# Forming the complex product with the filters outside TensorE, so that the way back takes one TensorE product per slot

## The chip, the cores and the metric

One core of a Trainium2 chip runs the kernel. The metric is the device time of one execution in microseconds, lower is better; a run's time is the median of its executions. A profile shows one execution, and its span is about 1.8 us shorter than the time of that execution, since it counts from the first to the last instruction. Times by stage below come from the profiles, totals from the timed runs. The profiled execution of the kernel before was some 3 us slower than its median, so differences of spans and of times are not quite the same.

## The reference

```python
# x (8, 3008, 256); filt_r, filt_i (1505, 256); w_in (256, 2048), w_out (2048, 256), both float64 in DRAM
X = np.fft.rfft(x, axis=1)
Y = X * (filt_r + 1j * filt_i)[None]
y = np.fft.irfft(Y, n=3008, axis=1).astype(np.float32).reshape(24064, 256)
h = y @ w_in
return ((h - np.tanh(h)) @ w_out).astype(np.float32)
```

It is a filter in the frequency domain along the sequence, then a dense layer with the function h - tanh(h) between its two matrices. All TensorE work is in float32.

## The kernel before

The sequence index is n = 47 q + r. The transform is one of length 64 over q ("first", product pf), a transposition through DRAM, then for each of 32 frequency slots a product over r (pz), the multiplication with the filters (uv), and a product back over b (pe), another transposition through DRAM, and the way back over a (pu). Real and imaginary parts lie side by side in the partitions: 47 + 47 = 94 rows. Four pairs of batches go through this; while the dense layers of one pair run (ph, po), the next pair's transforms stand between them. Only the first pair's have nothing to hide behind.

```python
    def load_a2(p, k):                                   # 94 rows from DRAM
        t = sb.tile([R2, BD], F32, tag="a2", bufs=2, name="a2")
        nc.sync.dma_start(t, dram(ct1[p], k * BD, [[NK * BD, R2], [1, BD]]))
        return t

    def middle(p):
        a2 = {0: load_a2(p, 0)}
        waiting = []

        def back():
            k, uv = waiting.pop(0)
            pe = ps.tile([128, 2, DM], F32, tag="z", bufs=2, name="pe")
            for f in range(2):                           # two products of the way back
                nc.tensor.matmul(pe[0:R2], g3[:, (2 * k + f) * R2:(2 * k + f + 1) * R2],
                                 uv[:, f], start=(f == 0), stop=(f == 1))
            e1 = sb.tile([R2, 2, DM], F32, tag="e1", bufs=2, name="e1")
            nc.scalar.copy(e1, pe[0:R2])
            nc.scalar.dma_start(
                dram(ct2[p], k * R2 * DM, [[DM, R2], [NQ * NR * DM, 2], [1, DM]]), e1)

        for k in range(NK):
            # ... next a2 is loaded ...
            pz = ps.tile([128, 2, DM], F32, tag="z", bufs=2, name="pz")
            nc.tensor.matmul(pz[0:R2], f2[:, k * R2:(k + 1) * R2], a2.pop(k),
                             start=True, stop=True)
            uv = sb.tile([R2, 2, 2, DM], F32, tag="uv", bufs=2, name="uv")
            for f in range(2):
                nc.vector.tensor_mul(
                    uv[:, f], pz[0:R2],
                    filt[:, f, k, :].unsqueeze(1).to_broadcast([R2, 2, DM]))
            waiting.append((k, uv))
            if len(waiting) > 1:
                back()
            yield

    # the start: the first pair's transforms, and the loads of what stays
    parts = [0, 4, 16, NK]
    for a, z in zip(parts, parts[1:]):
        nc.scalar.dma_start(f2[:, a * R2:z * R2], f2_d[:, a * R2:z * R2])
        nc.scalar.dma_start(g3[:, 2 * a * R2:2 * z * R2], g_d[:, 2 * a * R2:2 * z * R2])
        load_filters(a, z)                               # on GpSimd's queue
    for _ in fs[0]:
        pass
    # ...
    ws = weights()            # 32 jobs: load 128x256 float64 weights, convert them on VectorE
    for _ in ms[0]:
        next(ws, None)        # one conversion per slot, in the order of the text
```

## Time and profile before

| | before |
|---|---|
| time | 3473.27 us (3472.45 to 3473.28, 3 runs) |
| first stage, to the first product pz | 204.8 us |
| first pair's middle, from there to the first dense product ph | 265.1 us |
| from the first dense product to the end ("streaming stage") | 3004.6 us |

The last three rows are the stages. Their limits are read from the timeline of TensorE: the start of the first record of pz and of ph.

```profile
204.78 1.99 PE L269 MATMUL pz<-a,f_sb 94*94 94x512 f32 x2 [14.34 <-DMA a<-ct]
469.85 7.22 PE L311 MATMUL ph<-ut,w_in_sb 128*128 128x512 f32 x16
```

Columns are the start, the length, the engine and line, what it makes from what, the forms, the count of records, and in brackets how long the engine had been idle and what ended that. So at 204.78 TensorE had waited 14.34 us for the first load of a. The span of 3474.5 less 469.85 is the streaming stage. How the page of this kernel is read for its bounds is in the prediction.

### The profile page before, as it was taken

Reading aid. Unit: us, or ns where it says so; the run is one execution under the profiler, and the core shown is the slowest. Engines: PE = TensorE matmul, PEld = TensorE weight load, DVE = VectorE, ACT = ScalarE, POOL = GpSimd, SP = SyncE. Lnnn points to the kernel's source line nnn. Section 1 sums busy time; section 2 is a strip of 40 time slices with the busy share of each in tenths; the row PEclk is TensorE's granted clock in tenths of the full one; section 3 lists DMA queues with packets and bytes.
Section 4 is the critical chain, followed back from the end, with each engine's and each line's share of the span. In section 5 each row is a group of like instructions: output and inputs, shape, how many; then the busy total and the mean of one; then the engine's idle time right before and its main releaser. Section 6 shows DMA issues by size and latency. Waiting matters only on the chain. (4 is left out here: it accounts for less than half of the span.)

```text
span 3474.5 us, 36231 instructions
## 1 busy us (share of the span) xinstructions
PE 3219.2 (93%) x10800; PEld 1985.4 (57%) x10800; DVE 2744.9 (79%) x4466; ACT 1946.3 (56%) x3441; POOL 1333.2 (38%) x855
## 2 busy tenths in 40 slices
PE   1256689999999999999999999999999999999998
PEld 0011146666666666666666666666666666666665
DVE  2243158888888888888888888888888999999998
ACT  0000046665555666665555666665555666666665
POOL 2100024443333444443333444444333444445453
PEclk9955589999999999999999999999999999999999
DMA  5631122201111012201111112111111100000000
GB/s 116 143 119 63 50 80 73 69 26 47 43 45 37 32 54 85 63 29 48 47 41 34 32 59 86 47 37 41 48 40 36 35 17 19 19 19 19 17 13 11
DMA packets 107702, 168.44 MB, mean 48 GB/s; under 512 B 17120, under 2 KB 65992, under 8 KB 107124
## 3 DMA queue, kind: packets, MB, share of 16 engines
q1 hardware_dynamic: 37776, 82.39, 7.9%
q10 hardware_dynamic: 50496, 52.68, 4.5%
q0 software_dynamic: 19232, 31.04, 2.9%
q8 instruction: 85, 1.39, 0.2%
q14 instruction: 113, 0.93, 0.1%
HBM read 92.00 MB, written 73.92 MB: 48 GB/s over the span
## 5 line engine op out<-in xcount | busy, mean ns | idle before, releaser
L322 POOL TENSOR_SCALAR large<-u 128x512 uint8<-128x512 f32 (+1 forms) x768 | 1271.5, 1656 | 1973.3 <-ACT u L320 1933.1
L343 PE MATMUL po<-w_out_sb,gt 128*128 128x256 f32 x6016 | 1423.8, 380 | 11.3 <-ACT ot L350 7.4
L311 PE MATMUL ph<-ut,w_in_sb 128*128 128x512 f32 (+1 forms) x3072 | 1418.5, 583 | 0.0
L343 PEld LDWEIGHTS po<-w_out_sb,gt 128*128 128x128 f32 x6016 | 1138.2, 190 | 483.1 <-issue 283.9
L320 ACT ACTIVATE u<-ph 128x512 f32<-128x512 f32 (+1 forms) x768 | 451.6, 588 | 825.3 <-issue 301.0
L311 PEld LDWEIGHTS ph<-ut,w_in_sb 128*128 128x128 f32 x3072 | 578.0, 190 | 453.3 <-issue 399.7
L323 DVE TENSOR_TENSOR gt<-ph,u 128x512 f32<-128x512 f32 (+1 forms) x768 | 518.3, 675 | 272.3 <-ACT th L321 271.4
L330 DVE COPY_PREDICATED gt<-large,th 128x512 f32<-128x512 uint8 (+1 forms) x768 | 586.2, 763 | 68.2 <-DVE gt L327 2.7
L327 DVE SCALAR_TENSOR_TENSOR gt<-sb,gt 128x512 f32<-128x512 f32 (+1 forms) x768 | 539.6, 703 | 65.5 <-DVE gt L327 1.8
L326 ACT ACTIVATE sa<-u,bias 128x512 f32<-128x512 f32 (+1 forms) x768 | 548.8, 715 | 0.0
L326 ACT ACTIVATE sb<-u,bias 128x512 f32<-128x512 f32 (+1 forms) x768 | 546.4, 711 | 0.0
L327 DVE SCALAR_TENSOR_TENSOR gt<-sa,gt 128x512 f32<-128x512 f32 (+1 forms) x768 | 518.9, 676 | 0.0
L329 DVE TENSOR_TENSOR th<-ph,th 128x512 f32<-128x512 f32 (+1 forms) x768 | 513.4, 668 | 0.0
L321 ACT ACTIVATE th<-ph 128x512 f32<-128x512 f32 (+1 forms) x768 | 449.5, 585 | 0.0
L258 PE MATMUL pe<-uv,g_sb 94*94 94x512 f32 x512 | 299.5, 714 | 61.7 <-ACT e L261 60.8
L261 ACT COPY e<-pe 94x512 f32<-94x512 f32 x128 | 74.4, 581 | 406.8 <-PE pe L258 215.7
L273 DVE TENSOR_TENSOR uv<-pz,filt_sb 94x512 f32<-94x512 f32 x256 | 171.5, 680 | 164.1 <-PE pz L269 164.1
L237 PE MATMUL pf<-x_sb,wf_sb 128*128 128x512 f32 x192 | 121.4, 725 | 151.8 <-ACT a L239 134.4
L258 PEld LDWEIGHTS pe<-uv,g_sb 94*94 94x94 f32 x512 | 93.3, 188 | 242.4 <-issue 135.3
L269 PE MATMUL pz<-a,f_sb 94*94 94x512 f32 x256 | 160.1, 711 | 24.7 <-DMA a<-ct 19.8
L239 ACT COPY a<-pf 128x512 f32<-128x512 f32 x96 | 55.4, 577 | 200.8 <-DMA ct<-a 134.2
L237 PEld LDWEIGHTS pf<-x_sb,wf_sb 128*128 128x128 f32 x192 | 39.5, 224 | 198.0 <-ACT a L239 166.4
(34 smaller groups left out, 536.2 us busy)
## 6 DMA issues: line engine op xcount, KB each, us to landing
a<-ct SPq DMA_DIRECT2D x128, 188.0 KB
ct<-e ACTq DMA_DIRECT2D x128, 188.0 KB
x_sb<-in_x_dram SPq DMA_DIRECT2D x92, 256.0 KB
ct<-a ACTq DMA_DIRECT2D x92, 256.0 KB
e<-ct SPq DMA_DIRECT2D x44, 512.0 KB
out_dram<-ot POOLq DMA_DIRECT2D x44, 512.0 KB, 3.0
w<-in_moe_w_in_dram SPq DMA_DIRECT2D x16, 256.0 KB
w<-in_moe_w_out_dram SPq DMA_DIRECT2D x16, 256.0 KB
```

Source lines behind the costliest of these rows:

```text
L258: nc.tensor.matmul(pe[0:R2], g3[:, (2 * k + f) * R2:(2 * k + f + 1) * R2], uv[:, f], start=(f == 0), stop=(f == 1))
L273: nc.vector.tensor_mul(uv[:, f], pz[0:R2], filt[:, f, k, :].unsqueeze(1).to_broadcast([R2, 2, DM]))
L311: nc.tensor.matmul(ph[:, 0:n], w_in[:, h, t * 128:(t + 1) * 128], uts[i][:, h, 0:n], start=(h == 0), stop=(h == 1))
L320: nc.scalar.activation(u, ph, AF.Square)
L321: nc.scalar.activation(th, ph, AF.Tanh)
L322: nc.gpsimd.tensor_single_scalar(out=large, in_=u, scalar=SMALL, op=ALU.is_ge)
L323: nc.vector.tensor_mul(gt, ph, u)
L326: nc.scalar.activation(sq, u, AF.Square, bias=bias, scale=s)
L327: nc.vector.scalar_tensor_tensor(out=gt, in0=sq, scalar=v, in1=gt, op0=ALU.add, op1=ALU.mult)
L329: nc.vector.tensor_sub(th, ph, th)
L330: nc.vector.copy_predicated(gt, large, th)
L343: nc.tensor.matmul(po[i][:, j, :], gt[:, j * 128:(j + 1) * 128], w_out[:, t, :], start=(t == 0 and j % 2 == 0), stop=(t == NT - 1), skip_g ...
```

## The change

With Z = zr + i zi and F = fr + i fi, the kernel before let VectorE make all four real products (zr fr, zi fi, zr fi, zi fr) and TensorE add them up, with two matrices g for two operands. The change forms (zr fr - zi fi, zr fi + zi fr) first and lets TensorE multiply once. For this the parts move to partitions 0 and 64: ScalarE copies pz to zs, swapped and half negated, VectorE multiplies pz with fr, GpSimd multiplies zs with fi and adds the two. Padding partitions must not hold garbage, so the filters' padding is set to zero by VectorE ahead of the filter loads.

```diff
-    f2 = cst.tile([R2, NK * R2], F32, name="f2_sb")
-    g3 = cst.tile([R2, NK * 2 * R2], F32, name="g_sb")
+    f2 = cst.tile([R2, NK * 128], F32, name="f2_sb")
+    g3 = cst.tile([IM + NR, NK * R2], F32, name="g_sb")        # 111 rows, half the columns
-    filt = cst.tile([R2, 2, NK, DM], F32, name="filt_sb")
+    filt = cst.tile([128, 2, NK, DM], F32, name="filt_sb")
 ...
     def load_filters(a, z):
+        for p0 in (32, 96):
+            nc.vector.memset(filt[p0:p0 + 32, :, a:z, :], 0.0)
 ... (the filters' rows at partitions 0 and 64 in place of 0 and 47; the same bytes)
     def back():
-            for f in range(2):
-                nc.tensor.matmul(pe[0:R2], g3[:, (2 * k + f) * R2:(2 * k + f + 1) * R2],
-                                 uv[:, f], start=(f == 0), stop=(f == 1))
+            nc.tensor.matmul(pe[0:R2], g3[:, k * R2:(k + 1) * R2], uv[0:IM + NR],
+                             start=True, stop=True)
 ...
-            nc.tensor.matmul(pz[0:R2], f2[:, k * R2:(k + 1) * R2], a2.pop(k),
+            nc.tensor.matmul(pz, f2[:, k * 128:(k + 1) * 128], a2.pop(k),
                              start=True, stop=True)
-            uv = sb.tile([R2, 2, 2, DM], F32, tag="uv", bufs=2, name="uv")
-            for f in range(2):
-                nc.vector.tensor_mul(
-                    uv[:, f], pz[0:R2],
-                    filt[:, f, k, :].unsqueeze(1).to_broadcast([R2, 2, DM]))
+            uv = sb.tile([128, 2, DM], F32, tag="uv", bufs=2, name="uv")
+            zs = sb.tile([128, 2, DM], F32, tag="zs", bufs=2, name="zs")
+            both = [128, 2, DM]
+            nc.scalar.mul(zs[0:IM], pz[IM:128], -1.0)
+            nc.scalar.copy(zs[IM:128], pz[0:IM])
+            nc.vector.tensor_mul(uv, pz, filt[:, 0, k, :].unsqueeze(1).to_broadcast(both))
+            nc.gpsimd.tensor_mul(zs, zs, filt[:, 1, k, :].unsqueeze(1).to_broadcast(both))
+            nc.gpsimd.tensor_add(uv, uv, zs)
 ... (the constant matrices change to match; comments fall away)
```

More of the change, by code (lines that the diff above doesn't have):

```diff
@@ L26 @@
 HI = NR - LO
+IM = 64
 DFF = 2048
@@ L75, in _consts @@
     f2[31, 1::2, NR] = w32.real.T[:, HI]
+    f2w = np.zeros((NK, R2, 128))
+    f2w[:, :, 0:NR], f2w[:, :, IM:IM + NR] = f2[:, :, :NR], f2[:, :, NR:]
     ctw = np.exp(2j * np.pi * np.outer(np.arange(33), np.arange(NR)) / SEQ)
-    g = np.zeros((NK, 2, R2, R2))
+    g = np.zeros((NK, IM + NR, R2))
     for a in range(31):
@@ L82, in _consts @@
         tr, ti = t1.real.T[perm, :], t1.imag.T[perm, :]
-        g1, g2 = g[a, 0], g[a, 1]
-        g1[:NR, :NR], g1[:NR, NR:] = tr, ti
-        g1[NR:, :NR], g1[NR:, NR:] = -tr, -ti
-        g2[:NR, :NR], g2[:NR, NR:] = -ti, tr
-        g2[NR:, :NR], g2[NR:, NR:] = -ti, tr
-        g2[LO:NR, :] *= -1.0
-        g2[NR + LO:R2, :] *= -1.0
+        g[a, :NR, :NR], g[a, :NR, NR:] = tr, ti
+        g[a, IM:, :NR], g[a, IM:, NR:] = -ti, tr
+    g[:, IM + LO:] *= -1.0
     t0 = (wr.conj() * ctw[0][:, None] / SEQ).T
     t32 = (wr.conj() * ctw[32][:, None] / SEQ).T
-    g1, g2 = g[31, 0], g[31, 1]
-    g1[0, :NR] = t0.real[0]
-    g1[NR, NR:] = t32.real[HI]
-    g1[1:LO, :NR], g1[NR + 1:NR + LO, :NR] = 2 * t0.real[1:LO], -2 * t0.real[1:LO]
-    g2[1:LO, :NR], g2[NR + 1:NR + LO, :NR] = -2 * t0.imag[1:LO], -2 * t0.imag[1:LO]
-    g1[LO:NR, NR:], g1[NR + LO:R2, NR:] = 2 * t32.real[0:HI], -2 * t32.real[0:HI]
-    g2[LO:NR, NR:], g2[NR + LO:R2, NR:] = -2 * t32.imag[0:HI], -2 * t32.imag[0:HI]
+    g[31, 0, :NR] = t0.real[0]
+    g[31, IM, NR:] = t32.real[HI]
+    g[31, 1:LO, :NR], g[31, IM + 1:IM + LO, :NR] = 2 * t0.real[1:LO], -2 * t0.imag[1:LO]
+    g[31, LO:NR, NR:], g[31, IM + LO:, NR:] = 2 * t32.real[0:HI], -2 * t32.imag[0:HI]
     w = np.exp(2j * np.pi * np.outer(np.arange(NQ), np.arange(33)) / NQ)
@@ L112, in _consts @@
         wf1,
-        f2.transpose(1, 0, 2).reshape(R2, NK * R2),
-        g.transpose(2, 0, 1, 3).reshape(R2, NK * 2 * R2),
+        f2w.transpose(1, 0, 2).reshape(R2, NK * 128),
+        g.transpose(1, 0, 2).reshape(IM + NR, NK * R2),
         s2)]
@@ L154, in load_filters @@
         n = min(z, NK - 1) - a
-        for v, srcs in enumerate(((filt_r, filt_i), (filt_i, filt_r))):
-            for p0, src in zip((0, NR), srcs):
+        for p0 in (32, 96):
+            nc.vector.memset(filt[p0:p0 + 32, :, a:z, :], 0.0)
+        if z == NK:
+            for p0 in (0, IM):
+                nc.vector.memset(filt[p0:p0 + 1, 1, NK - 1], 0.0)
+        for v, src in enumerate((filt_r, filt_i)):
+            for p0 in (0, IM):
                 nc.gpsimd.dma_start(
@@ L162, in load_filters @@
                     dram(src.tensor, (NQ - 1 - a) * DM, [[NQ * DM, HI], [-DM, n], [1, DM]]))
-            if z < NK:
-                continue
-            k = NK - 1
-            p_re, p_im = (0, NR) if v == 0 else (NR, 0)
-            nc.gpsimd.dma_start(filt[p_re:p_re + LO, v, k, :],
-                                dram(filt_r.tensor, 0, [[NQ * DM, LO], [1, DM]]))
-            nc.gpsimd.dma_start(filt[p_im:p_im + 1, v, k, :],
-                                dram(filt_r.tensor, SEQ // 2 * DM, [[DM, 1], [1, DM]]))
-            nc.gpsimd.dma_start(filt[p_im + 1:p_im + LO, v, k, :],
-                                dram(filt_i.tensor, NQ * DM, [[NQ * DM, LO - 1], [1, DM]]))
-            for p0, src in ((p_re, filt_r), (p_im, filt_i)):
+                if z < NK:
+                    continue
+                k = NK - 1
+                nc.gpsimd.dma_start(filt[p0 + 1:p0 + LO, v, k, :],
+                                    dram(src.tensor, NQ * DM, [[NQ * DM, LO - 1], [1, DM]]))
                 nc.gpsimd.dma_start(filt[p0 + LO:p0 + NR, v, k, :],
                                     dram(src.tensor, NQ // 2 * DM, [[NQ * DM, HI], [1, DM]]))
+                if v == 0:
+                    nc.gpsimd.dma_start(
+                        filt[p0:p0 + 1, v, k, :],
+                        dram(src.tensor, (SEQ // 2 if p0 else 0) * DM, [[DM, 1], [1, DM]]))
     biases = []
@@ L360 @@
     for a, z in zip(parts, parts[1:]):
-        nc.scalar.dma_start(f2[:, a * R2:z * R2], f2_d[:, a * R2:z * R2])
-        nc.scalar.dma_start(g3[:, 2 * a * R2:2 * z * R2], g_d[:, 2 * a * R2:2 * z * R2])
+        nc.scalar.dma_start(f2[:, a * 128:z * 128], f2_d[:, a * 128:z * 128])
+        nc.scalar.dma_start(g3[:, a * R2:z * R2], g_d[:, a * R2:z * R2])
         load_filters(a, z)
```

## The prediction

> **What bounds the kernel now.** I read the page's first two parts, then a table of stretches, then the groups of one stretch, then the waits of the start. The page and the stretches (columns: from:to and length, busy time and count for PE, PEld, DVE, ACT, POOL, then granted clock, share of the 16 DMA engines, GB/s):
>
> ```profile
> PE 3219.2 (93%) x10800; PEld 1985.4 (57%) x10800; DVE 2744.9 (79%) x4466; ACT 1946.3 (56%) x3441; POOL 1333.2 (38%) x855
> ...
> 0.00:60.00 60.00, 6.17 (x6) 1.51 (x6) 11.66 (x41) 2.02 (x3) 15.83 (x19) 1.00 0.58 116
> 60.00:100.00 40.00, 4.15 (x4) 1.01 (x4) 11.34 (x41) 1.02 (x2) 2.55 (x2) 1.00 0.40 117
> 100.00:198.00 98.00, 34.83 (x38) 9.15 (x38) 33.75 (x121) 12.08 (x21) 17.66 (x18) 0.96 0.69 172
> 198.00:470.00 272.00, 186.74 (x223) 55.39 (x224) 70.89 (x184) 22.59 (x39) 0.00 (x0) 0.51 0.21 71
> 470.00:800.00 330.00, 328.31 (x1156) 211.27 (x1155) 288.70 (x441) 217.73 (x381) 146.14 (x91) 1.00 0.17 53
> 800.00:1000.00 200.00, 200.00 (x679) 122.05 (x678) 165.28 (x259) 117.54 (x205) 77.03 (x48) 1.00 0.13 43
> 1000.00:2800.00 1800.00, 1794.76 (x6274) 1140.39 (x6273) 1535.00 (x2420) 1127.22 (x2003) 747.66 (x478) 1.00 0.14 46
> 2800.00:3474.00 674.00, 664.26 (x2427) 444.67 (x2425) 628.27 (x963) 446.10 (x791) 326.31 (x202) 1.00 0.05 17
> ```
>
> There are four stages: the first pair's transform over q (to about 198 us), the first pair's middle (198 to 470), the dense layers of pairs 0 to 2 with the next pair's transforms between them (470 to about 2800), and the last pair's dense layers alone. TensorE is busy without a gap from 470 on, at the full clock. Busy is not peak, so I check with the groups of 800 to 1000 us:
>
> ```profile
> L311 PE MATMUL ph<-ut,w_in_sb 128*128 128x512 f32 x180 | 84.8, 592 | 0.0
> L343 PE MATMUL po<-w_out_sb,gt 128*128 128x256 f32 x357 | 84.4, 379 | 0.0
> L258 PE MATMUL pe<-uv,g_sb 94*94 94x512 f32 x62 | 29.2, 592 | 0.0
> L269 PE MATMUL pz<-a,f_sb 94*94 94x512 f32 x32 | 16.4, 592 | 0.0
> L301 PE MATMUL pu<-s_sb,e 128*128 128x128 f32 x48 | 6.6, 280 | 0.0
> ```
>
> Each float32 product shows as two records (62 records for 31 products of the way back). Records overlap, so their mean of 592 ns isn't their price. The chain that ended last gives the price in a stream: four ph records in 1.72 us (430 ns each, 860 ns per product of 512 columns), eight po records in 1.73 us (216 ns), and so 108 ns for 128 columns. Then 180 x 0.430 + 357 x 0.216 + 94 x 0.430 + 48 x 0.108 = 200.1 us of 200. TensorE streams all the time; what it sheds here comes off the time.
>
> In the first pair's middle it is different:
>
> ```profile
> ACT e L261 <- DMA ct<-e: 191.0, 25, 10.8
> DVE uv L273 <- PE pz L269: 157.7, 29, 8.6
> ...
> 414.03 0.58 ACT L261 COPY e<-pe 94x512 f32<-94x512 f32 x1 [7.17 <-DMA ct<-e]
> 414.67 3.73 PE L258 MATMUL pe<-uv,g_sb 94*94 94x512 f32 x4 [2.32 <-ACT e L261]
> 418.19 1.92 PE L269 MATMUL pz<-a,f_sb 94*94 94x512 f32 x2
> 421.81 0.58 ACT L261 COPY e<-pe 94x512 f32<-94x512 f32 x1 [7.20 <-DMA ct<-e]
> ```
>
> (waits between 200 and 440 us: total, times, longest; then two slots of the timeline). A slot takes 7.8 us though TensorE works 5.4 us of it at half clock: the copy of a result waits until the store of two slots earlier has landed and given up its buffer. The store sets the pace, not TensorE.
>
> **What the Trainium skill says.**
> - "TensorE: Matmul & The Clock Gate", section "Back-to-back issue gap": a warm product costs N/2.4 + 2.5 ns, 216 ns at 512 columns; columns streamed count, not rows or stationary width. The trace agrees: 430 ns per record is two such passes, and 94-row and 128-row groups have the same mean of 592 ns. Part 1 there gives a half clock to an array that isn't kept busy; the column of 0.51 in the first middle agrees.
> - "GPSIMD Engine Reference", section 3.1: a two-input float32 elementwise instruction takes 4497 ns at 2048 elements, about 2.6 cycles per element, and section 1 says its SBUF interfaces are shared with VectorE. By that slope I estimate 1.2 us for 512 elements undisturbed. No two-input GpSimd instruction is in this trace; its one-input compare takes 1656 ns on the mean, so I plan with 1.2 to 2.0 us.
> - "DMA: Bandwidth & Descriptors", section "Why a DMA increments its semaphore by 16 and not by 1": a transfer is spread over the largest k up to 16 that divides the slowest dimension of both sides, and on the hardware queues these are the lowest-numbered engines; its table gives about 27 GiB/s per engine. 94 rows give k = 2. The trace fits: 188 KB in and 188 KB out per 7.8 us are 48 GB/s, and at 360 to 420 us the DMA share is 0.13, that is 2.1 of 16 engines.
>
> **The change part by part.**
>
> TensorE: one of two g products per slot goes, 128 in all, 32 for each of four pairs. 96 of them lie in the streaming stage: 96 x 0.86 = 82.6 us off. The other 32 lie in the first middle, behind the stores: about 0. The forward product is now 128 columns wide in its stationary operand instead of 94, which doesn't alter the 512 columns streamed; its weight load (about 160 to 190 ns) stays beside the stream.
>
> VectorE: one product instead of two per slot, 680 ns less; 128 x 0.68 = 87 us of busy time, off the critical path, worth nothing by itself. It leaves room (VectorE is 83% busy at 800 to 1000 us).
>
> ScalarE: two copies per slot of 64 partitions, negated and swapped. The copy of e (94x512) takes 581 ns, so about 1.16 us per slot, 149 us in all. A slot comes every three steps: 3 x 3.445 us dense + 0.86 + 0.86 = 12.1 us of TensorE after the change. ScalarE has then 12 activations (4 x 3; nominally 7.8 us), one e copy and the two new ones: 9.5 us of 12.1. They come right behind pz, at a time when ScalarE now waits (before, it idled 1.95 us ahead of the e copy).
>
> GpSimd: two more instructions per slot, 2.4 to 4 us, beside three compares of 1.66 us: 7.4 to 9 us of 12.1. In program order they stand between two compares. From the timeline of 866 to 872 us: pz ends about 0.9 us after it starts, copies 1.2 us, product and sum to about 4.5 to 6 us after the start of pz; the next step's compare could begin at about 4.3 us, so it slips by up to 2 us. Its reader, the predicated copy, stands over 3 us behind it in VectorE's order. The way back takes uv one slot (12 us) later. So nothing new reaches TensorE.
>
> The loads at the start: g goes from 94 rows of 6016 words to 111 rows of 3008 (2.26 MB on two DMA engines to 1.34 MB on k = 3), f2 grows from 1.13 to 1.54 MB, still k = 2. Bytes on each of the two crowded engines: (2.26 + 1.13)/2 = 1.70 MB before, 1.34/3 + 1.54/2 = 1.22 MB after, 0.48 MB less. The first stage does look held by these engines: ScalarE could not issue until 60 us, and only two chunks passed from 60 to 100 us. At the 24 GB/s per engine that the middle shows, 0.48 MB is up to 20 us. Against it stand new VectorE memsets of the filters' padding, ahead of the filter loads: 32768 elements, 34 us at one element per 0.96 GHz cycle (an estimate from the 680 ns of the 512-element products), while VectorE is almost idle and TensorE waits anyway. The filters load later by some microseconds but those of slot 16 on are needed only after 330 us. I take 9 us of gain from the first stage.
>
> Sum: 82.6 + 9 = 91.6 us, less about 2 us for new stalls: 3473.3 - 90 = 3383 us.
>
> **The rivals.**
> 1. GpSimd or its shared port becomes the wait: contended instructions of 3 us and more would give 11 us or more per slot of 12.1, predicated copies would wait and TensorE with them. For: the predicated copy lasts 0.97 to 1.14 us where it lies over a compare against 0.71 alone, so the two do hinder each other; VectorE is 83 to 90% busy. Against: VectorE loses 680 ns per slot in exchange, and there are three compares per slot already. If it came: some 40 us of gain lost, 3425 us.
> 2. VectorE becomes the bound as TensorE gets shorter: 188 steps per pair with five operations, started about 0.64 us apart, give 3.2 us against TensorE's 3.445. After a slot it has 3 x 3.2 + 0.65 = 10.3 of 12.1 us. It would cost only if its operations stretched by 15%. The last pair, all dense, already runs with VectorE 93% busy and TensorE at its pace.
> 3. The first stage gets worse: memsets delay weight conversions and filter loads, and x loads queue behind weight loads. TensorE and ScalarE stand still until 60 us anyway. If it came: 10 to 20 us lost, about 3400 us.
> 4. The start gains nothing and nothing else changes: 3391 us.
> 5. All 128 products count (110 us): only if the first middle followed TensorE. The store waits speak against it; 3360 us.
>
> **Range and chances.** The middle is 82.6 us, certain within some 5% as it rests on a stage that streams to 100%; the start may be anywhere from -10 to +20. So 3367 to 3399 us holds eight times in ten. A gain of 2% needs about 69 us: it fails if rival 1 comes, or if the start loses over 13 us. I give 0.89 to faster, 0.10 to the same, 0.01 to slower.
>
> **What would show it.** Right: the streaming stage without gaps, the group of the way back with half the records (256), each stretch from one pair to the next shorter by 27.5 us (32 x 0.86), the last pair unchanged near 670 us, the first middle again at 7.8 us per slot with ScalarE waiting for the store, GpSimd's new instructions between 1.2 and 2.0 us. Wrong: TensorE waiting for the predicated copy or for GpSimd's sum in the streaming stage; a first middle paced by GpSimd; a first stage that ends later than 198 us (memsets) or more than 20 us earlier.

## The result, and the profile after

The changed kernel takes 3408.69 us (3408.01 to 3410.55, 4 runs) against 3473.28 us for the kernel before on the same chip: a ratio of 0.9814, with a 95% interval of 0.98 to 0.9828. Ratios here are the mean time of one kernel's runs over that of the other's of the same rounds, so not quite the ratio of the medians. The gain is 65 us where 90 were forecast, and the time lies above the range of 3367 to 3399.

The same two lines of TensorE's timeline, for the changed kernel:

```profile
171.87 2.05 PE L268 MATMUL pz<-a,f_sb 94*128 94x512 f32 x2 [13.37 <-DMA a<-ct]
483.96 2.44 PE L314 MATMUL ph<-ut,w_in_sb 128*128 128x512 f32 x5
```

| stage, us | before | after | difference | forecast |
|---|---|---|---|---|
| first stage | 204.8 | 171.9 | -32.9 | -9 |
| first pair's middle | 265.1 | 312.1 | +47.0 | 0 |
| streaming stage | 3004.6 | 2923.3 | -81.3 | -82.6 + 2 |
| span | 3474.5 | 3407.3 | -67.2 | -90 |

The streaming stage did what was forecast. The start, taken together, was to gain 9 us and lost 14.1. First the part that went right: the stretches of the changed kernel (columns as in the prediction: from:to and length, busy time and count of PE, PEld, DVE, ACT, POOL, granted clock, DMA share, GB/s), and groups of 800 to 1000 us (busy time and mean, then idle time ahead).

```profile
198.00:470.00 272.00, 110.37 (x124) 30.78 (x124) 63.35 (x202) 54.35 (x93) 76.44 (x60) 0.55 0.18 59
...
484.00:800.00 316.00, 314.52 (x1114) 203.54 (x1113) 279.21 (x422) 216.20 (x378) 154.43 (x96) 1.00 0.16 53
800.00:1000.00 200.00, 200.00 (x694) 126.40 (x693) 177.38 (x263) 144.97 (x252) 129.23 (x84) 1.00 0.15 50
1000.00:2700.00 1700.00, 1695.35 (x5992) 1096.28 (x5991) 1518.59 (x2287) 1192.31 (x2106) 956.66 (x617) 1.00 0.15 48
```

```profile
L333 DVE COPY_PREDICATED gt<-large,th 128x512 f32<-128x512 uint8 x48 | 44.1, 918 | 3.3
...
L278 POOL TENSOR_TENSOR uv<-uv,zs 128x512 f32<-128x512 f32 x16 | 25.2, 1573 | 1.2
L277 POOL TENSOR_TENSOR zs<-zs,filt_sb 128x512 f32<-128x512 f32 x17 | 22.5, 1326 | 24.1 <-ACT zs L275 24.1
L268 PE MATMUL pz<-a,f_sb 94*128 94x512 f32 x32 | 16.4, 592 | 0.0
L257 PE MATMUL pe<-uv,g_sb 111*94 111x512 f32 x32 | 16.4, 591 | 0.0
```

TensorE still has no gap. In 200 us it now gets through 386 po records against 357, and 32 pe records against 62. GpSimd's busy time rises from 77.0 to 129.2 us and is nowhere near the bound. Its two new instructions take 1326 and 1573 ns, inside the planned 1.2 to 2.0 us. They do cost VectorE something: the predicated copy goes from 766 ns to 918 ns on the mean in this stretch (763 to 823 over the whole run), but VectorE has the room.

Now the part that went wrong. The timeline of the changed kernel from the first slots on, other lines left out (SPq and ACTq are the queues from which SyncE and ScalarE issue transfers):

```profile
183.70 1.91 PE L268 MATMUL pz<-a,f_sb 94*128 94x512 f32 x2
183.94 0.58 ACT L260 COPY e<-pe 94x512 f32<-94x512 f32 x1 [4.93 <-PE pe L257]
185.16 10.55 SPq L193 DMA_DIRECT2D w<-in_moe_w_in_dram  x5
185.40 1.68 PE L257 MATMUL pe<-uv,g_sb 111*94 111x512 f32 x2
197.80 42.98 SPq L193 DMA_DIRECT2D w<-in_moe_w_out_dram  x16
220.72 0.27 ACTq L261 DMA_DIRECT2D ct<-e  x1
221.09 0.59 ACT L274 ACTIVATE zs<-pz 64x512 f32<-64x512 f32 x1 [36.56 <-DMA w<-in_moe_w_out_dram]
...
246.16 0.42 DVE L220 TENSOR_TENSOR w_out_sb<-ft,pt 128x256 f32<-128x256 f32 x1
246.50 1.28 DVE L276 TENSOR_TENSOR uv<-pz,filt_sb 128x512 f32<-128x512 f32 x2
```

Two slots pass, the second pe ends at 187, and the third pe comes at 248.65. In between VectorE does nothing but weight conversions (36.0 us busy of the 37 from 185 to 222, 19.3 of the 24.5 from there on), and its product for the third slot, whose pz was there at 185.6, stands behind all of them, at 246.50. The loads of a stand behind the weight loads likewise. ScalarE stands still for 36.6 us in the meantime: the store of the first e, ready at 184.5, was issued at 220.72, and the profile puts the end of that wait down to a weight load. In the built program this store waits for a DMA semaphore that is handed on from one transfer to another.

The instruction order of VectorE, read from the built kernels, shows the same without a chip. M is a memset, a dot is the first instruction of one of the 32 conversions, U a product of a slot (two per slot before, one after):

```
before  ......................UUUU.UUUU.UU.UUUU.UUUU.UUUU.UUUU.UU.UUUU.U.UUUUUUUU...
after   MMMMMMMM.........U.U......................UUUUU...
```

Before, 22 conversions stood in the first stage and the rest came one by one between slots. After, 9 stand in the first stage and 22 in one lump between the second and the third slot. That explains two things at once: a first stage free of most weight loads, and a middle with a hole of some 60 us. But both readings come from one kernel, in which five things changed. So they were tested.

### The profile page after: what moved, and what is told of

Its sections match the earlier page's. It is cut to its first block, busy times and chain, and to the rows that moved or that the text cites. A ratio compares the mean times of both kernels' runs of the same rounds, so it can differ in the third digit from the quotient of the medians.

```text
span 3407.3 us, 36312 instructions
## 1 busy us (share of the span) xinstructions
PE 3079.5 (90%) x10544; PEld 1942.0 (57%) x10544; DVE 2768.3 (81%) x4346; ACT 2097.2 (62%) x3697; POOL 1697.7 (50%) x1111
## 4 chain that ended last, share of the span: by engine, by line
PE 79%; DMA 11%; DVE 5%; issue 2%; ACT 1%; POOL 0%; ACTq 0%; DVEq 0%; POOLq 0%; SPq 0%
PE po L346 35%; PE ph L314 35%; DMA ct<-e 6%; DMA ct<-a 4%; PE pe L257 3%; PE pz L268 2%; DVE gt L330 2%; PE pu L304 2%; PE pf L237 2%; DMA w<-in_moe_w_in_dram 1%; DVE gt L326 1%; DMA w<-in_moe_w_out_dram 1%; ACTq L364 0%; POOL large L325 0%; DMA x_sb<-in_x_dram 0%
## 5 line engine op out<-in xcount | busy, mean ns | idle before, releaser
L346 PEld LDWEIGHTS po<-w_out_sb,gt 128*128 128x128 f32 x6016 | 1138.1, 190 | 484.2 <-issue 262.3
L333 DVE COPY_PREDICATED gt<-large,th 128x512 f32<-128x512 uint8 (+1 forms) x768 | 632.3, 823 | 71.5 <-DVE gt L330 4.1
L330 DVE SCALAR_TENSOR_TENSOR gt<-sb,gt 128x512 f32<-128x512 f32 (+1 forms) x768 | 552.0, 719 | 73.6 <-DVE gt L330 0.9
L330 DVE SCALAR_TENSOR_TENSOR gt<-sa,gt 128x512 f32<-128x512 f32 (+1 forms) x768 | 528.2, 688 | 0.0
L277 POOL TENSOR_TENSOR zs<-zs,filt_sb 128x512 f32<-128x512 f32 x128 | 170.4, 1331 | 370.2 <-ACT zs L275 370.2
L268 PE MATMUL pz<-a,f_sb 94*128 94x512 f32 x256 | 160.8, 714 | 159.6 <-ACT e L260 139.3
L276 DVE TENSOR_TENSOR uv<-pz,filt_sb 128x512 f32<-128x512 f32 x128 | 88.0, 688 | 193.9 <-ACT zs L275 190.8
L278 POOL TENSOR_TENSOR uv<-uv,zs 128x512 f32<-128x512 f32 x128 | 191.8, 1498 | 55.7 <-DVE uv L276 47.4
L257 PE MATMUL pe<-uv,g_sb 111*94 111x512 f32 x256 | 157.5, 701 | 30.8 <-POOL uv L278 30.8
L268 PEld LDWEIGHTS pz<-a,f_sb 94*128 94x128 f32 x256 | 51.6, 217 | 215.5 <-ACT e L260 183.7
L274 ACT ACTIVATE zs<-pz 64x512 f32<-64x512 f32 x128 | 76.1, 594 | 145.4 <-PE pz L268 103.4
```

The costliest lines, as they stand in the source:

```text
L257: nc.tensor.matmul(pe[0:R2], g3[:, k * R2:(k + 1) * R2], uv[0:IM + NR], start=True, stop=True)
L268: nc.tensor.matmul(pz, f2[:, k * 128:(k + 1) * 128], a2.pop(k), start=True, stop=True)
L330: nc.vector.scalar_tensor_tensor(out=gt, in0=sq, scalar=v, in1=gt, op0=ALU.add, op1=ALU.mult)
L333: nc.vector.copy_predicated(gt, large, th)
L346: nc.tensor.matmul(po[i][:, j, :], gt[:, j * 128:(j + 1) * 128], w_out[:, t, :], start=(t == 0 and j % 2 == 0), stop=(t == NT - 1), skip_g ...
```

## The experiments

The theory: the start is ruled by the place of the conversions in the order of VectorE and of the load queue, and the change moved them twice, by its memsets (out of the first stage) and by putting GpSimd into the chain of a slot (into a lump). Rivals: the memsets' own time costs the start; ScalarE's and GpSimd's new work is slow in the first middle; the lighter g alone explains the shorter first stage; and, for the streaming stage, that all 128 removed products count, or that the new work eats part of the gain.

Stages of all runs, in us; "ahead" is the number of conversions ahead of the first slot, the next column the longest lump after it:

| run | time | first stage | first middle | streaming | ahead | lump |
|---|---|---|---|---|---|---|
| before | 3473.3 | 204.8 | 265.1 | 3004.6 | 22 | 1 |
| after | 3408.7 | 171.9 | 312.1 | 2923.3 | 9 | 22 |
| e1_pool_memset | 3395.1 | 186.8 | 283.0 | 2923.9 | 22 | 10 |
| e8_dve_pair0 | 3372.4 | 172.1 | 274.1 | 2923.9 | 9 | 1 |
| e9_dve_pair0_pool_memset | 3394.2 | 185.3 | 276.5 | 2930.2 | 22 | 2 |
| e2_before_memset | 3472.5 | 191.3 | 275.0 | 3004.9 | 11 | 1 |
| e15_one_per_slot | 3378.5 | 169.8 | 280.3 | 2926.2 | 2 | 2 |
| e14_late_filters | 3400.1 | 142.1 | 329.7 | 2926.5 | 10 | 16 |
| e3_before_one_product | 3388.5 | 202.5 | 263.5 | 2919.6 | 22 | 1 |
| e11_before_split | 3391.2 | 198.7 | 180.7 | 3008.7 | 22 | 1 |
| e13_before_split_gf | 3435.1 | 170.8 | 262.3 | 3003.0 | 28 | 1 |
| e12_e8_split | 3201.9 | 145.8 | 132.0 | 2930.8 | 14 | 1 |
| e10_dve0_split | 3239.1 | 170.5 | 134.0 | 2928.4 | 26 | 2 |
| e16_tie_split | 3258.2 | 137.8 | 185.2 | 2935.1 | 2 | 2 |

All results were correct except e3's. The expectation texts count some conversions up to three off; the table has the counts of the built orders.

### e1_pool_memset: the memsets on GpSimd

```diff
-            nc.vector.memset(filt[p0:p0 + 32, :, a:z, :], 0.0)
+            nc.gpsimd.memset(filt[p0:p0 + 32, :, a:z, :], 0.0)
```
(the single rows of the last slot likewise)

> The changed kernel with the memsets of the filters' padding on GpSimd instead of VectorE. Order theory (the lost start is a matter of where the 32 weight conversions stand in VectorE's and the load queue's order): by the built order 22 conversions now stand ahead of the first slot and 10 between slots 2 and 3, in place of 9 and 21. The stall between slots 2 and 3 should shrink from 63 us to about 27, but the first stage should again carry weight loads and end later than 172 us, near 185. Dense layers from about 477 us (484 in the changed kernel), total near 3400 us. Rival (the memsets themselves cost the start, by VectorE time or by the shared port): 34 us or more gained, 3375 or less. Rival (the new ScalarE and GpSimd work paces the slots): no change, 3409.

3395.12 us, ratio to before 0.9771. The first product pz came at 186.8 us (185 expected), the dense layers began at 469.8 (477 expected). With 10 conversions in the lump in place of 22, the first middle is 29.1 us shorter; with 22 in the first stage in place of 9, that stage is 14.9 us longer. The time went where the conversions went. The rival that the memsets' own time costs the start, which gave 3375 or less, is out: they went off VectorE, and the total fell by 13.6 us and not by 34 or more.

### e8_dve_pair0: the first pair's product and sum on VectorE

```diff
-            nc.gpsimd.tensor_mul(zs, zs, filt[:, 1, k, :].unsqueeze(1).to_broadcast(both))
-            nc.gpsimd.tensor_add(uv, uv, zs)
+            eng = nc.vector if p == 0 else nc.gpsimd
+            eng.tensor_mul(zs, zs, filt[:, 1, k, :].unsqueeze(1).to_broadcast(both))
+            eng.tensor_add(uv, uv, zs)
```

> The changed kernel with the product and the sum of the first pair alone on VectorE instead of GpSimd; memsets stay on VectorE. In the built order the conversions are then spread one by one between the slots. Order theory: first stage still ends at about 172 us, no stall after slot 2, slots at about 8 us since each now carries a weight load; dense layers from about 450 us, total near 3374 us. Rival (the memsets cost the start): no gain, 3409. Rival (GpSimd is slow in the first pair's chain, not the order): a gain too, but spread over all slots, with the stall after slot 2 left.

3372.37 us (3374 expected), ratio 0.9708. The first stage is unchanged at 172.1 us and the middle 38 us shorter than in the changed kernel. This is faster than both kernels, by an edit that gives VectorE more work. By itself it can't tell an order from a slow GpSimd, as it takes away both; e15 does.

### e9_dve_pair0_pool_memset: both edits

> Both edits: memsets on GpSimd, first pair's product and sum on VectorE. The built order is then close to that of the kernel before (22 conversions ahead of slot 1, the rest spread). Order theory: first stage as in the kernel before or some 10 us shorter for the lighter g (first forward product at 190 to 200 us), no stall; dense layers from 455 to 465 us; total 3378 to 3388 us, which is what the prediction gave for an unchanged start. Rival (something else in the change costs the start): above 3400.

3394.18 us, ratio 0.9771: 6 us above the expected 3378 to 3388. First stage (185.3, a little under the expected 190 to 200) and dense start (461.8, expected 455 to 465) agree. The excess is in the streaming stage, 2930.2 against 2923.9 in e8, where TensorE's waits for the copy that empties po are 12.8 us against 8.0; the rest of it wasn't looked into. Against e8 it shows that getting the memsets off VectorE is no gain: it brings the conversions back into the first stage.

### e2_before_memset: the kernel before, with memsets on VectorE

```diff
         n = min(z, NK - 1) - a
+        for p0, p1 in ((32, 64), (64, R2)):
+            nc.vector.memset(filt[p0:p1, :, a:z, :], 0.0)
```

> The kernel before with memsets on VectorE of the same size as in the change, ahead of its filter loads (they are overwritten by the loads). The g matrices are still the heavy ones. Built order: 8 weight loads ahead of the first slot in place of 22, the rest spread over the slots, no lump. If the 33 us that the changed kernel's first stage gained come from the weight loads that left it: first forward product near 175 us, total some 10 to 25 us below 3473. If they come from the lighter g: near 205 us, total about 3473 to 3480.

3472.46 us, ratio 0.9993 (interval 0.9976 to 1.001): no gain in sum, where 10 to 25 us were expected. The first stage did get shorter, from 204.8 to 191.3, but not to the expected 175, and the middle gave 9.9 us of it back, as the weight loads moved into it.

With this run the two causes of the shorter first stage separate:

| first stage, us | 22 conversions ahead | 9 to 11 ahead |
|---|---|---|
| heavy g (2.26 MB on 94 rows) | 204.8 (before) | 191.3 (e2) |
| light g (1.34 MB on 111 rows) | 186.8 (e1) | 171.9 (after) |

The lighter loads are worth 18.0 to 19.4 us, the missing conversions 13.5 to 14.9 us; the sum is the 32.9 us of the result. Neither alone explains it. (The memsets, on VectorE in e2 and on GpSimd in e1, also change when the filter loads start; that was not separated from the conversions.)

### e15_one_per_slot: the order made even, GpSimd kept

The conversions' float tile takes its buffers from the ring of uv, so conversions and slots have to take turns. No other line changes, but 2 conversions now stand ahead of the first slot in place of 9.

```diff
-            ft = sb.tile([128, 256], F32, tag="sa", bufs=2, name="ft")
+            ft = sb.tile([128, 2, DM], F32, tag="uv", bufs=4, name="ft")[:, 0, :]
...
-            uv = sb.tile([128, 2, DM], F32, tag="uv", bufs=2, name="uv")
+            uv = sb.tile([128, 2, DM], F32, tag="uv", bufs=4, name="uv")
```

```
after      MMMMMMMM.........U.U......................UUUUU...
e15        MMMMMMMM..UU..UUU..UU.U.U.U.U.U.U.U.U.U.U.U.U.U.U.U.U.U.U.U.U.U.U.U.U.U.
```

> The changed kernel with one edit: the conversions' float tile takes its buffer from the ring that uv uses (4 buffers in place of 2), so that conversions and slots have to take turns. GpSimd keeps the first pair's product and sum, VectorE the memsets, the filter loads their place. In the built order there is then one conversion per slot and no lump. Order theory: no long gap, first forward product near 165 to 172 us, slots of about 8.2 us (each carries a weight load), dense layers from about 445 us, total 3360 to 3380. Rival (GpSimd's or ScalarE's work in the first middle is slow by itself): gaps or slow slots stay, total near 3409.

3378.53 us, ratio 0.9724, inside the expected 3360 to 3380. The hole is gone. The waits from 175 to 440 us (total, times, longest):

```profile
PE pz L268 <- ACT e L260: 126.3, 28, 7.6
ACT e L260 <- DMA ct<-e: 126.0, 28, 7.4
```

No wait is longer than 9.2 us, and ScalarE's copy of e waits for the store of e 28 times: the store paces the slots again, as before the change. GpSimd, ScalarE's copies and the memsets are all still there. So the order is shown to be the cause of the loss of the changed kernel, and the rival of a slow chain is out for this kernel. (The edit also makes the ring of uv larger; e8 closes the hole without that.)

### e14_late_filters: another way to move the lump

```diff
+        if a < 16:
-        load_filters(a, z)
+            load_filters(a, z)
...
-    for _ in ms[0]:
+    for k, _ in enumerate(ms[0]):
+        if k == 1:
+            load_filters(16, NK)
         next(ws, None)
```

> The changed kernel with only the last part of the filter loads (slots 16 to 31) issued from within the first middle instead of ahead of it; GpSimd keeps the first pair's product and sum and VectorE the memsets. In the built order the conversions now stand 9 ahead of slot 1, 5 between slots 2 and 3, 1 between 3 and 4, 16 between 4 and 5. Order theory: the long gap moves with them: about 13 us between the results of slots 2 and 3 and some 40 us between those of 4 and 5, in place of 67 us around slots 1 to 3. Total 3390 to 3412. Rival (GpSimd is slow at its start, a first use or a wait of its own): the gap stays between slots 2 and 3.

3400.12 us, inside the expected 3390 to 3412, but the gaps were not the forecast ones: 40.2 us between the copies of e of slots 2 and 3 (13 expected), then 28.6 us to slot 4 and 27.8 us from there to slot 5 (some 40 expected for this last one). The timeline of GpSimd shows why:

```profile
187.53 0.51 POOL L160 DMA_DIRECT2D filt_sb<-in_filt_i_dram  x1 [0.18 <-issue]
188.31 2.56 POOL L163 DMA_DIRECT2D filt_sb<-in_filt_i_dram  x1 [0.27 <-issue]
190.86 0.52 POOL L169 DMA_DIRECT2D filt_sb<-in_filt_i_dram  x1
191.37 0.52 POOL L171 DMA_DIRECT2D filt_sb<-in_filt_i_dram  x1
191.91 2.49 POOL L277 TENSOR_TENSOR zs<-zs,filt_sb 128x512 f32<-128x512 f32 x2
```

The late filter loads stood in GpSimd's own queue, ahead of the product of the third slot, which had its operand since 157 us. One of them waited 19 us for an earlier filter transfer. So the edit made a new wait of the same kind on another engine, and the run can't decide what it was made for. It does show that the first stage falls to 142.1 us once those filter loads are out of it.

### e3_before_one_product: the removed TensorE work alone

```diff
-            for f in range(2):
-                nc.tensor.matmul(pe[0:R2], g3[:, (2 * k + f) * R2:(2 * k + f + 1) * R2],
-                                 uv[:, f], start=(f == 0), stop=(f == 1))
+            nc.tensor.matmul(pe[0:R2], g3[:, 2 * k * R2:(2 * k + 1) * R2],
+                             uv[:, 0], start=True, stop=True)
```

> The kernel before with the second product of the way back simply left out (a wrong result on purpose); all else as before. TensorE theory: the stage from the first dense product to the end, 3004.6 us in the kernel before, gets 96 x 0.86 = 82.6 us shorter (about 2922; 2923.3 in the changed kernel), and the first pair's middle does not change because the stores pace it: total 3388 to 3394 us. Rival (all 128 products count): 3363. Rival (the changed kernel's ScalarE and GpSimd work eats part of the gain in the streaming stage): this kernel's stage would be clearly shorter than 2923.

3388.46 us, ratio 0.9755. The streaming stage is 2919.6 us, 85.0 less than before (82.6 expected), and the first middle 263.5 us, 1.6 less than before: the 32 products of the first pair are indeed worth nothing there. The changed kernel's streaming stage is 3.7 us longer than this one, by one profile each; so its extra work on ScalarE and GpSimd costs no more than a few us there.

### e11_before_split and e13_before_split_gf: how many DMA engines carry the 94 rows

In e11 the loads of a and the stores of e of the kernel before are cut into 80 + 14 rows; in e13 only the loads of f2 and g are.

```diff
-        nc.sync.dma_start(t, dram(ct1[p], k * BD, [[NK * BD, R2], [1, BD]]))
+        for q0, q1 in ((0, 80), (80, R2)):
+            nc.sync.dma_start(t[q0:q1], dram(ct1[p], (k + q0 * NK) * BD,
+                                             [[NK * BD, q1 - q0], [1, BD]]))
```
(the store of e, and in e13 the loads of f2 and g, in the same way)

> The kernel before, with the loads of a and the stores of e, 94 rows each, cut into 80 + 14 rows, so that the row counts divide by 16 and by 14 in place of 2. If two crowded DMA engines pace the first pair's middle (7.8 us per slot), the slot should fall to about 5 us, where TensorE at half clock is next: first middle from 265 to about 180 us, total 3380 to 3400. Rival (latency of a store, whatever its engines): slot stays at 7.8 us and total at 3473.

> The kernel before, with only the loads of f2 and g cut into 80 + 14 rows. If the first stage of the kernel before is held by two engines that carry the heavy g and f2 (1.70 MB each), the first forward product starts well before 204.8 us, at 180 to 187 as in the kernels with the light g; total about 3450 to 3460 us. Rival (the bytes of g count, not their engines): 200 us and 3470 or more.

e11 takes 3391.22 us (ratio 0.9761) and e13 3435.06 us (ratio 0.9888). Without a byte less to move, e11's first middle falls from 265.1 to 180.7 us, as expected, and e13's first stage from 204.8 to 170.8 us, more than expected. The slots of e11, by its copies of e:

```profile
221.88 0.58 ACT L263 COPY e<-pe 94x512 f32<-94x512 f32 x1 [4.54 <-PE pe L260]
227.00 0.58 ACT L263 COPY e<-pe 94x512 f32<-94x512 f32 x1 [4.54 <-PE pe L260]
```

A slot takes 5.12 us in place of 7.8 and the copy waits for TensorE, not for a store. The DMA share rises from 0.13 (360 to 420 us, before) to 0.38. So the row count of the transfers, and with it the number of engines, paced the kernel before at its start, and not the latency of a store. e13 had 28 conversions ahead of the first slot and still a first stage as short as the changed kernel's: so most of what the conversions and the heavy g cost there came with the undivided loads of f2 and g. It is not a general rule for conversions, as e10 below shows.

### e12_e8_split, e10_dve0_split, e16_tie_split: the faster versions

e12 is e8 with all transfers of 94 and 111 rows cut so (80 + 14 and 96 + 15); e10 has the memsets on GpSimd in addition; e16 is e15 with the same cuts.

> Candidate for the fastest: the changed kernel with the first pair's product and sum on VectorE (3372 us), and all transfers of 94 and 111 rows (f2, g, a, e) cut so that they spread over 14 to 16 engines. If two crowded engines set the pace, the slots of the first middle fall from 8 to about 5 us and the first stage ends some 10 us earlier: total 3260 to 3300 us. Rival (latency): 3372.

> The fastest so far (3202 us: first pair's product and sum on VectorE, transfers cut so that they spread over 14 to 16 engines) with the memsets on GpSimd as well. 26 conversions then stand ahead of slot 1 in place of 14. Order theory: first stage some 5 to 15 us longer than 146 us, slots at TensorE's or ScalarE's pace a little earlier; total 3195 to 3220. It tells whether the memsets' place matters once the transfers are spread.

> The same edit with the transfers of 94 and 111 rows cut so that they spread over 14 to 16 engines, with GpSimd kept in the first pair. If spread transfers and an even order are all that counts, it comes within 30 us of the 3202 us of the version with VectorE in the first pair: 3185 to 3230. If GpSimd in the chain of a slot costs when stores no longer pace the slots, it is slower than that.

e12 takes 3201.92 us (3193.98 to 3210.4), ratio 0.9209 to the kernel before: 272 us off, more than the expected 3260 to 3300, and faster than both kernels of this case. One stretch of e11 and of e12, in this order:

```profile
200.00:275.00 75.00, 74.63 (x88) 24.07 (x87) 39.66 (x115) 8.13 (x14) 0.00 (x0) 0.50 0.38 105
```

```profile
200.00:275.00 75.00, 50.54 (x96) 13.62 (x96) 64.24 (x177) 35.68 (x61) 0.00 (x0) 0.98 0.59 169
```

In e11 TensorE is busy all through at a granted clock of 0.50; in e12 it is busy two thirds of the time at 0.98. I had expected slots of 5 us in e12. They took 4.45 us up to 190 us, at a clock of 0.50, and 3.3 us after that, when TensorE had left the half clock. What makes the clock rise in one and not in the other was not tested.

e10 (3239.09, expected 3195 to 3220) has a first stage of 170.5 us against 145.8: with 26 conversions ahead of the first slot in place of 14, and the memsets in GpSimd's queue among the filter loads, the stage costs 25 us more, where 5 to 15 were expected, even with spread transfers. Which of the two it is was not separated. e16 (3258.23, expected 3185 to 3230) is the second alternative of its expectation: once stores no longer pace the slots, a slot with GpSimd in its chain takes 5.3 us against 3.3. The same stretch of e16, and two instructions of the conversions in it:

```profile
200.00:275.00 75.00, 58.84 (x58) 13.02 (x58) 74.41 (x161) 24.80 (x43) 37.62 (x29) 0.50 0.45 126
L209 DVE TENSOR_SCALAR it<-w 128x256 int32<-128x256 int32 x15 | 20.2, 1349 | 0.0
L218 DVE SCALAR_TENSOR_TENSOR pt<-pt,it 128x256 int32<-128x256 int32 x14 | 16.8, 1199 | 0.4
```

The chain itself need not be all of the 2 us. TensorE stayed at the half clock, where e12's slots took 4.45 us; and VectorE is full, as these two instructions, which lie beside GpSimd's, take 1349 and 1199 ns on the mean against 312 and 441 in e12 from 200 to 265 us, where GpSimd stands still. How the 2 us divide was not tested. In e15, at 8.4 us a slot on the mean, ScalarE's waits for the stores hide all this.

## Why the prediction was right or wrong, point by point

- **The streaming stage** (96 products at 0.86 us, 82.6 us). Right, in mechanism and size: 81.3 us in the changed kernel and 85.0 with the products alone left out (e3). The prices taken from the chain of waits held.
- **The first pair's 32 products are worth nothing.** Right: 1.6 us in e3.
- **GpSimd and its shared port** (rival 1). Rightly set aside: instructions of 1326 and 1573 ns where 1.2 to 2.0 us were planned. The hindrance is there, 60 ns per predicated copy over the run, and costs no more than the few us between e3 and the changed kernel (3.7 us, one profile each). VectorE did not become the bound either (rival 2).
- **The loads at the start** ("I take 9 us of gain from the first stage"). The term was too small: 32.9 us came. 18.0 to 19.4 of them are the lighter g, near the full 20 us that the estimate had before it was cut down; 13.5 to 14.9 are conversions that left the stage. Rival 3 (memsets make the first stage worse) went the other way. The memsets did take the estimated 34 us (they ended at 35.7 us), though 680 ns per 512 elements, which the prediction names as the source, would give 43.5.
- **"The first middle again at 7.8 us per slot."** This step failed, and it alone turned the forecast. The pace of a slot in the later part was right, 7.9 us on the mean from the fifth copy of e at 259.05 to the one at 456.29, 25 slots later. But the middle took 47.0 us more, in the hole between slots 2 and 3. The prediction had checked each engine's new work against the pace of a slot and had not looked at the order of VectorE in the first middle, although the order of the built kernel showed 22 conversions in front of the third slot's product before any run. It took the conversions for a background that stays where it is. They were placed anew.
- **The sum.** Forecast -82.6 - 9 + 2 = -90; measured -81.3 - 32.9 + 47.0 = -67.2 in the profiles. That the first stage gave 24 us more than forecast was luck; it hid half of what the failed step cost. Even against a start that gains nothing (3391 us, the fourth rival), the result is 18 us worse. e8 and e15, with the order made even by two different edits, land at 3372 and 3379 us, inside the predicted range.

Why the scheduler made the lump is argued, not shown. The lump goes when GpSimd leaves the first pair's slots (e8), and GpSimd's queue holds all filter loads ahead of its first product; so the scheduler's model may have held GpSimd busy with them, the third slot late, and VectorE free for conversions. On the chip GpSimd was free: its first product began at 175.22 us, right after the copies that it waited for.

## What to carry to other kernels

Where a scheduler sets the order of the engines, a change in one place can move work that it doesn't touch; compare the built orders of before and after in every stage, above all where a queue works in order and nothing hides a wait. When work is moved off the bound, price the removed work in the stage where that engine streams, and treat the unhidden start as a sum of its own. Look at the row counts of transfers that set a pace: cutting 94 rows into 80 + 14 took 83 us off the kernel before (e11), more than the change itself.

## What the Trainium skill lacked or had wrong

- "DMA: Bandwidth & Descriptors", section "Why a DMA increments its semaphore by 16 and not by 1": its rule for the number of engines held (2 engines for 94 rows), but it doesn't say that transfers of such shapes then crowd the same lowest engines and set the pace while the mean DMA share is low (0.13 at 360 to 420 us). Cutting the rows brought the first middle from 265.1 to 180.7 us (e11) and the first stage from 204.8 to 170.8 us (e13).
- "TensorE: Matmul & The Clock Gate", Part 1: the clock is said to rise to full after a busy window of some 3.4 us. In e11 TensorE was busy 74.63 of 75 us at a granted clock of 0.50, with a product every 1.7 us, which is twice the 0.86 of the stream, so it had no gaps; in e12 it was busy 50.54 of 75 us at 0.98. The rule as told doesn't give both.
- "GPSIMD Engine Reference", section 3.1: the slope gives 1.1 us for a two-input instruction of 512 elements (an estimate from that page, which the prediction took up to 1.2); measured 1.26 us where VectorE stood nearly idle (both instructions at 415 to 419 us of the changed kernel), and 1326 ns for the product and 1573 ns for the sum beside a busy VectorE.
- No page tells that the order which a scheduler builds may put unrelated work in front of a waiting instruction: 22 conversions, 61 us of VectorE, in front of the third slot here.
